# An mLSTM cell and a mixture of depths on one core: gates on 96 partitions, other places in a step, another order of the tail

## The chip, the core and the metric

The kernel runs on one core of one Trainium2 chip, in float32. A core has five engines that run their own instruction streams: TensorE (PE, matmuls into PSUM), VectorE (DVE), ScalarE (ACT), GpSimd (POOL) and SyncE (SP, which here only issues DMAs). The metric is the device time of the kernel in microseconds, the median of several runs; lower is better.

## The reference

Two blocks follow each other. The first is an mLSTM cell over batch 4, 8 heads, 768 positions and head size 40. In each position t it keeps a running maximum m of the gates, a matrix C and a vector n per head:

```python
m_new = np.maximum(f_gate[:, :, t] + m, i_gate[:, :, t])
f_stab = np.exp(f_gate[:, :, t] + m - m_new)
i_stab = np.exp(i_gate[:, :, t] - m_new)
C = f_stab * C + i_stab * outer(v, k)
n = f_stab * n + i_stab * k
y[t] = sigmoid(o_gate[t]) * (C @ q) / max(|n @ q|, 1)
```

The second block is a mixture of depths. Each batch has 768 rows of 8 x 40 = 320 numbers. A score per row (row times w_gate) picks the 128 highest rows of each batch; those alone go through two layers (320 to 1024 with ReLU, 1024 to 320), are scaled by the sigmoid of their score and added to the row. All other rows pass unchanged:

```python
top_idx = np.argpartition(-scores[b], capacity)[:capacity]
h = np.maximum(x[b, top_idx] @ w1, 0.0)
out[b, top_idx] = x[b, top_idx] + sigmoid(scores[b, top_idx])[:, None] * (h @ w2)
```

## The kernel before

**Tiling.** `_fast` (L27) treats 256 positions of one batch as a step: N = 12 steps n, three (s = 0, 1, 2) for each batch b. All 8 heads of a step are done together; inside a step the positions lie in four pieces of 64 (two chunks c of 128 partitions, two halves r). The order of the instructions on each engine is the order in which the program writes them; nothing reorders it. SP, PE, DVE, ACT and POOL each work through their own part of that order and wait for each other by semaphores. `_general` (L614) is a fallback for other numbers and isn't run here.

**A step.** For step n the loop (L524) holds: `load(n + 3)` (L527), DMAs of v, k and q three steps ahead and of o two steps ahead, all on SP; `store(n - 1)` of finished rows to `out`, on SP too; `scores(n)` (L262, PE), `masked(n)` (L274, DVE); `update(n + 1)` (L230, PE, into the one buffer pU), `states(n + 1)` (L242, DVE, running sums of C); `widen` (L202, ACT, spreads q to 64 columns a head); `weigh(n + 2)` (L219, POOL, v times the gate columns into `wv`); `turn` (L206, PE transposes of k or q, ACT copies out of PSUM); `read(n)` (L281, PE, state times q into pH), `attend(n)` (L298, PE, adds scores times `wv` to pH), `divide(n)` (L307, DVE, gives y), `sigmoid` (ACT) and `output(n)` (L320, POOL, y times o into x). `router(n - 1)` (L335, DVE) makes the scores of the second block.

**Gates.** `gate_sums`, `gate_rows`, `gate_cols` (L158, L166, L181) make, for one s, the decays of all 32 pairs of batch and head on 32 partitions: two scans of 256 on DVE, an Exp on ACT, then five small matmuls that turn the rows into columns `cols[s]`. The three s go one after the other: the maximum that one leaves (`m`) starts the next scan. They lie partly ahead of the loop and partly in step 0.

**Second block.** For batch b-1, one batch behind: `spread` (L363, PE and ACT) puts all scores on every partition; `ranks` (L385) counts for each row how many scores are greater, three counts on DVE (`greater`) and three on ACT (`signs`); `select` (L413, DVE) makes the one-hot `sel`; `numbers` (L451, PE `pi`, then DVE `index`) turns it into row numbers; `fetch` (L459) gathers these rows from `out` by an indirect DMA on POOL, and `fetched` (L466) transposes them; `layer1` (L480), `layer2` (L491, ending with the scaled copy `yg` on ACT and an indirect DMA on POOL that adds `yg` to `out`). In a batch's step s = 1 there are ranks, select, numbers and fetch of the batch before (and layer 2 of the one before that); in s = 2 there are fetched and layer 1. The last batch takes its rows with a one-hot matmul from x in SBUF (`picked`, L429), and its counts are made in two parts (`ranks_first`, `ranks_last`), because its last third comes late.

**Tail.** After the loop: score of the last step, layers of batch 2, ranks, `picked`, layers of batch 3. Just before layer 2 of batch 3 all engines read a flag `good` (L608) that decides on the fallback.

**PSUM.** Pools `ps_s` (one buffer of two banks: scores, spread), `ps_u` (one of two banks: pU), `ps_t` (two of one bank: transposes, `ph`, `py`, `pi`, `pX`, gate columns), `ps_h` (one of two banks: pH).

Of the kernel before, what the change touches and what calls it, by code (L numbers as in the profile page):

```python
# [16 lines left out]
BIG = 1.0e30  # L17
# [9 lines left out]
def _fast(ctx, tc, q, k, v, i_gate, f_gate, o_gate, w_gate, w1_in, w2_in, out):  # L27
# [11 lines left out]
    WARM = 18  # L39
# [16 lines left out]
    f_sb = gate.tile([BH, S], FP, name="f_sb")  # L56
    i_sb = gate.tile([BH, S], FP, name="i_sb")

    def load(n):

        if n < N:
            b, s = divmod(n, NS)
            for t, src in ((v_t, v), (k_t, k)):
                for c in range(2):
                    a = s * 256 + c * 128
                    SP.dma_start(out=t[n % NB][:, c, :, 0:D], in_=src[b, :, a:a + 128, :].rearrange("h p d -> p h d"))
            SP.dma_start(out=q_t[n % NB], in_=q[b, :, 256 * s:256 * s + 256, :].rearrange("h (p t) d -> p h (t d)", t=2))
        n -= 1
        if 0 <= n < N:
            b, s = divmod(n, NS)  # L70
            for r in range(2):
                for c in range(2):
                    a = s * 256 + c * 128 + r * 64
                    SP.dma_start(out=o_t[n % NO][64 * c:64 * c + 64, r],
                                 in_=o_gate[b, :, a:a + 64, :].rearrange("h p d -> p h d"))

    SP.dma_start(out=f_sb, in_=f_gate.rearrange("b h s -> (b h) s"))
    SP.dma_start(out=i_sb, in_=i_gate.rearrange("b h s -> (b h) s"))
    hot = const.tile([128, 128], FP, name="hot")
    DVE.memset(hot, 1.0)  # L80
    one = gate.tile([BH, 256], FP, name="one")
    DVE.memset(one, 1.0)
    m = gate.tile([BH, NS + 1], FP, name="m")
    DVE.memset(m[:, 0:1], -BIG)
    flags = gate.tile([128, NS + B], FP, name="flags")
# [4 lines left out]
    load(0)  # L90
    wg = const.tile([128, DM], FP, name="wg")
    SP.dma_start(out=wg, in_=_bcast(w_gate, 128))
    load(1)
# [17 lines left out]
    odd = gate.tile([BH, 2], FP, name="odd")  # L111
    for j in range(2):
        DVE.tensor_reduce(out=odd[:, j:j + 1], in_=ident[0:BH, j:BH:2], axis=AX.X, op=OP.add)
    pairs = gate.tile([BH, BH // 2], FP, name="pairs")
    DVE.tensor_tensor(out=pairs, in0=ident[0:BH, 0:BH:2], in1=ident[0:BH, 1:BH:2], op=OP.add)
# [38 lines left out]
    cols = []  # L154

    rowed = {}

    def gate_sums(s):  # L158
        own = slice(256 * s, 256 * s + 256)
        F = gate.tile([BH, 256], FP, name="F", tag="F")  # L160
        a = gate.tile([BH, 256], FP, name="a", tag="a")
        DVE.tensor_tensor_scan(out=F, data0=one, data1=f_sb[:, own], initial=0.0, op0=OP.mult, op1=OP.add)
        DVE.tensor_tensor(out=a, in0=i_sb[:, own], in1=F, op=OP.subtract)
        rowed[s] = F, a

    def gate_rows(s):  # L166
        F, a = rowed[s]
        carry = m[:, s:s + 1]
        M = gate.tile([BH, 256], FP, name="M", tag="M")
        E = gate.tile([BH, 514], FP, name=f"E{s}")  # L170
        DVE.tensor_tensor_scan(out=M, data0=one, data1=a, initial=carry, op0=OP.mult, op1=OP.max)
        DVE.tensor_scalar(out=E[:, 256:512], in0=a, scalar1=M[:, 255:256], scalar2=None, op0=OP.subtract)
        DVE.tensor_tensor(out=E[:, 512:513], in0=carry, in1=M[:, 255:256], op=OP.subtract)
        DVE.tensor_scalar(out=E[:, 0:256].rearrange("b (r c t) -> b c r t", r=2, c=2),
                          in0=M.rearrange("b (c r t) -> b c r t", c=2, r=2), scalar1=M[:, 255:256], scalar2=None,
                          op0=OP.subtract)
        DVE.tensor_tensor(out=m[:, s + 1:s + 2], in0=F[:, 255:256], in1=M[:, 255:256], op=OP.add)
        ACT.activation(out=E[:, 0:513], in_=E[:, 0:513], func=AF.Exp)
        rowed[s] = E

    def gate_cols(s):  # L181
        E = rowed[s]
        dz = gate.tile([BH, 128], FP, name=f"dz{s}")
        DVE.tensor_scalar(out=dz.rearrange("b (j e) -> b j e", j=2), in0=odd.unsqueeze(2).to_broadcast([BH, 2, 64]),
                          scalar1=E[:, 512:513], scalar2=None, op0=OP.mult)
        DVE.tensor_scalar(out=flags[0:BH, s:s + 1], in0=E[:, 0:1], scalar1=LEAST, scalar2=None, op0=OP.is_ge)
        pc = ps_t.tile([128, 5, BH], FP, name="pc", tag="t")
        for j in range(4):
            e = (256, 384, 0, 128)[j]
            PE.transpose(pc[:, j, :], E[:, e:e + 128], ident[0:BH, 0:BH])  # L190
        PE.matmul(pc[:, 4, 0:BH // 2], dz, pairs, start=True, stop=True)
        cols.append(const.tile([128, 5, BH], FP, name=f"cols{s}"))
        DVE.tensor_copy(out=cols[s][:, 0:2, :], in_=pc[:, 0:2, :])  # L193
        for r in range(2):
            DVE.tensor_copy(out=cols[s][:, 2 + r, :].rearrange("s (b j p) -> s b j p", j=2, p=NP),
                            in_=pc[:, 2 + r, :].rearrange("s (b p j) -> s b j p", j=2, p=NP))
        DVE.tensor_copy(out=cols[s][:, 4, 0:BH // 2], in_=pc[:, 4, 0:BH // 2])
# [8 lines left out]
    def turn(n, name):  # L206
        T = work.tile([128, NP, 256], FP, name=name)
        for c in range(2):
            src = k_t[n % NB] if name == "kT" else qw_t[n % 2]
            pt = ps_t.tile([128, NP, 128], FP, name="pt", tag="t")  # L210
            for p in range(NP):
                PE.transpose(pt[:, p, :], src[:, c, 2 * p:2 * p + 2, :].rearrange("s j d -> s (j d)"), ident)  # L212
            if name == "kT":
                ACT.copy(out=T[:, :, 128 * c:128 * c + 128], in_=pt)  # L214
            else:
                ACT.copy(out=T.rearrange("e p (u t) -> e t p u", t=2)[:, c], in_=pt)  # L216
        pending[n][name] = T

    def weigh(n):  # L219
        pending[n] = {}  # L220
        b, s = divmod(n, NS)
        for r in range(2):
            o = slice(64 * r, 64 * r + 64)
            POOL.tensor_tensor(out=wv_t[n % 3][o, :, :, r], in0=v_t[n % NB][o], op=OP.mult,  # L224
                               in1=cols[s][o, 0:2, b * H:b * H + H].unsqueeze(3).to_broadcast([64, 2, H, D1]))
# [193 lines left out]
    def index(b, hi, lo, count):  # L419
# [6 lines left out]
        DVE.tensor_scalar(out=flags[:, NS + b:NS + b + 1], in0=count, scalar1=1.0, scalar2=None, op0=OP.is_equal)  # L426
        dep[b]["idx"] = idx

    def picked(b):  # L429
# [6 lines left out]
        pX = ps_t.tile([128, 3, 128], FP, name="pX", tag="t")  # L436
        d["xeT"] = mod.tile([128, 3, 128], FP, name="xeT")
        for j in range(3):
            for r in range(2 * NS):
                PE.matmul(pX[:, j, :], x[:, r, 128 * j:128 * j + 128], sel[:, r, :], start=(r == 0), stop=(r == 2 * NS - 1))  # L440
            ACT.copy(out=d["xeT"][:, j], in_=pX[:, j])
# [49 lines left out]
    def layer2(b, f0=0, f1=NF):  # L491
# [5 lines left out]
        if f1 < NF:  # L497
            return
        dep.pop(b)
# [7 lines left out]
    gate_sums(0)  # L507
    gate_rows(0)
    gate_sums(1)
    causal()  # L510
    gate_cols(0)
    weigh(0)
    zero(wv_t[2].rearrange("s c h r x -> s c h (r x)"))
    zero(k_t[2][:, :, :, D:DP])
    turn(0, "kT")
    gate_rows(1)
    widen(0)
    update(0)
    turn(0, "qT")
    gate_cols(1)  # L520
    weigh(1)
    gate_sums(2)
    scores(0)
    for n in range(N):  # L524
        b, s = divmod(n, NS)
        more = n + 1 < N
        load(n + 3)  # L527
# [8 lines left out]
        if n > 0:  # L536
            scores(n)
        masked(n)
        if n == 0:
            states(0)  # L540
            gate_rows(2)
        if b > 1 and s == 1:
            layer2(b - 2)
        if n > 0 and (s < 2 or not more):
            router(n - 1)
        if b > 0 and s == 1:
            ranks(b - 1)
            select(b - 1)
        if more:
            update(n + 1)  # L550
            states(n + 1, 0, 4 if n else 3)
            widen(n + 1)
        if n > 0 and n + 2 < N:
            weigh(n + 2)
        if n > 0 and s == 2 and more:
# [3 lines left out]
        if not more:  # L559
            sigmoid(n)  # L560
            gated(n)
        read(n)
        if b > 0 and s == 1:
            numbers(b - 1)
            fetch(b - 1)
        if n == 0:
            gate_cols(2)
            states(1, 3)
            weigh(2)
            tables()  # L570
        if more:
# [4 lines left out]
            if b > 0 and s == 2:  # L576
                fetched(b - 1)
                layer1(b - 1, 0)
                layer1(b - 1, 4)
        else:  # L580
            dep[b] = {"sb4": spread(b, 0, 4)}
            ranks_first(b)
        attend(n)
        divide(n)
        if more:
            output(n)
        if n == 1:
            margins()
    b = B - 1
    router_last(N - 1)  # L590
    output(N - 1)
    fetched(b - 1)
    layer1(b - 1, 0)
    ranks_last(b)
    store(N - 1)
    layer1(b - 1, 4)
    layer2(b - 1)
    picked(b)
    layer1(b, 0)
    layer1(b, 4)  # L600
    picked_numbers(b)
    good = gate.tile([1, 1], I32, name="good")
    pg = ps_s.tile([1, NS + B], FP, name="pg", tag="s")
# [3 lines left out]
    DVE.tensor_scalar(out=good, in0=total, scalar1=float(NS * BH + 128 * B), scalar2=None, op0=OP.is_equal)  # L607
    value = nc.values_load(good[0:1, 0:1], min_val=0, max_val=1)  # L608
    layer2(b)
# [352 lines left out]
```

## Time and profile before

| | us |
|---|---|
| median of 3 runs | 196.38 |
| lowest and highest | 194.38, 197.03 |
| the profiled execution | 198.05 |
| its span, first to last instruction | 196.1 |
| PE busy | 157.8 |
| DVE busy | 106.2 |
| ACT busy | 77.9 |
| POOL busy | 72.0 |

The span is divided on the page into 40 slices of 4.9 us, with one digit for each: the busy share of an engine in tenths, or the clock granted to PE. A line of a timeline gives start, duration, engine, line of the program, operation, output and input, how many instructions are merged, and in brackets how long the engine stood idle before and what ended that. A matmul in float32 shows as two records. The loads have short rows: of 93606 DMA packets 88352 are under 512 bytes. The DMA queue of SP carries 22.65 MB. The chain of work that ended last is 57% PE, 9% ACT, 8% DMA and 7% DVE.

### The profile page before, as it was taken

How to read it: one execution, taken by the hardware profiler on the slowest of the kernel's cores; microseconds unless marked ns; L12 is line 12 of the kernel's file. 1: busy time of each engine (PE TensorE's matmuls, PEld its weight loads, DVE VectorE, ACT ScalarE, POOL GpSimd, SP SyncE). 2: the span in 40 equal slices, each digit the busy share in tenths (PEclk: the TensorE clock that was granted, in tenths of full speed). 3: DMA queues.
4: the chain of work that ended last, by engine and by line, in shares of the span. 5: the costliest groups of instructions: out<-in, count | busy, mean ns of one | idle time of the engine just before them, and what ended most of it. 6: DMA issues, size and time to landing. Idle time of an engine off the chain costs nothing.

```text
span 196.1 us, 6660 instructions
## 1 busy us (share of the span) xinstructions
PE 157.8 (80%) x2857; PEld 138.3 (71%) x2857; DVE 106.2 (54%) x269; ACT 77.9 (40%) x142; POOL 72.0 (37%) x89
## 2 busy tenths in 40 slices
PE   7866499998972980899996998999958759989650
PEld 7765489987961870899975787998748559779420
DVE  5747857869598255008796293297855583200100
ACT  8731158553761331132519534242463445211110
POOL 4235029699362026205335480092312540030030
PEclk9975589999996698599999699999988979999996
DMA  5999999859788978998799889720221202020002
GB/s 110 197 183 149 184 181 156 158 120 178 161 137 183 301 126 169 310 192 163 126 165 188 163 202 156 157 67 5 70 33 37 70 4 62 5 33 0 7 10 37
DMA packets 93606, 24.31 MB, mean 124 GB/s; under 512 B 88352, under 2 KB 93088, under 8 KB 93568
## 3 DMA queue, kind: packets, MB, share of 16 engines
q1 hardware_dynamic: 92848, 22.65, 61.0%
q0 software_dynamic: 720, 1.15, 3.6%
q8 instruction: 24, 0.39, 0.9%
q14 instruction: 14, 0.11, 0.2%
HBM read 19.20 MB, written 4.59 MB: 121 GB/s over the span
## 4 chain that ended last, share of the span: by engine, by line
PE 57%; issue 9%; ACT 9%; DMA 8%; DVE 7%; SPq 4%; POOL 2%; POOLq 0%; ACTq 0%; DVEq 0%
PE ph L487 13%; PE pt L212 9%; PE py L496 7%; PE pH L303 7%; PE pU L238 5%; PE pS L271 4%; ACT sgn L383 4%; DMA v<-in_v_dram 4%; PE pH L293 3%; PE warm L89 3%; DMA xe<-out_dram,idx 3%; PE pX L440 2%; PE pB L368 2%; DMA o<-in_o_gate_dram 2%; POOL wv L224 1%
## 5 line engine op out<-in xcount | busy, mean ns | idle before, releaser
L224 POOL TENSOR_TENSOR wv<-v,cols 64x656 f32<-64x656 f32 x24 | 34.3, 1428 | 25.7 <-DVE cols L193 19.6
L325 POOL TENSOR_TENSOR x<-y,o 128x320 f32<-128x320 f32 x24 | 20.7, 882 | 42.4 <-issue 18.8
L487 PE MATMUL ph<-xeT,w 128*128 128x128 f32 x192 | 26.4, 304 | 4.2 <-ACT xeT L472 4.2
L487 PEld LDWEIGHTS ph<-xeT,w 128*128 128x128 f32 x192 | 25.6, 218 | 5.2 <-ACT xeT L472 5.1
L340 DVE CUSTOM_DVE_ANT_0 scr<-x,wg 128x320 f32<-128x320 f32 x22 | 22.4, 1018 | 4.7 <-POOL x L325 3.0
L238 PE MATMUL pU<-wv,k 128*64 128x82 f32 x384 | 17.7, 249 | 7.0 <-issue 4.2
L216 ACT COPY qT<-pt 128x512 f32<-128x512 f32 x24 | 14.2, 628 | 21.3 <-PE pt L212 21.2
L238 PEld LDWEIGHTS pU<-wv,k 128*64 128x64 f32 x384 | 15.6, 146 | 8.9 <-issue 5.3
L312 DVE SCALAR_TENSOR_TENSOR den<-pH,cols 128x16 f32<-128x16 f32 x12 | 2.1, 175 | 35.8 <-PE pH L303 35.8
L214 ACT COPY kT<-pt 128x512 f32<-128x512 f32 x24 | 13.0, 585 | 20.6 <-PE pt L212 20.5
L496 PE MATMUL py<-w,hT 128*128 128x320 f32 x64 | 18.2, 437 | 1.0 <-DVE good L607 1.0
L303 PE MATMUL pH<-wv,P 128*64 128x82 f32 x384 | 18.8, 258 | 0.0
L502 POOL DMA_INDIRECT out_dram<-yg,idx x4 | 6.3, 1585 | 33.7 <-ACT yg L501 30.7
L303 PEld LDWEIGHTS pH<-wv,P 128*64 128x64 f32 x384 | 16.8, 155 | 2.2 <-issue 1.5
L212 PE MATMUL pt<-ident,qw 128*128 128x128 f32 x96 | 16.9, 322 | 1.8 <-DVE flags L426 0.7
L496 PEld LDWEIGHTS py<-w,hT 128*128 128x128 f32 x64 | 11.8, 190 | 5.6 <-issue 1.0
L212 PEld LDWEIGHTS pt<-ident,qw 128*128 128x128 f32 x96 | 12.1, 161 | 3.9 <-PE pt L212 1.7
L271 PE MATMUL pS<-qT,kT 40*64 40x64 f32 x768 | 14.8, 229 | 0.0
L293 PE MATMUL pH<-C,qT 40*64 40x41 f32 x704 | 13.9, 229 | 0.9 <-DVE y L317 0.6
L277 DVE TENSOR_TENSOR P<-pS,mask 128x1024 f32<-128x1024 f32 x12 | 14.6, 1213 | 0.0
L293 PEld LDWEIGHTS pH<-C,qT 40*64 40x64 f32 x704 | 12.4, 134 | 3.0 <-issue 2.3
L250 DVE TENSOR_TENSOR C<-pU,C 128x164 f32<-128x164 f32 x40 | 13.1, 326 | 1.9 <-PE pU L238 0.8
(106 smaller groups left out, 214.2 us busy)
## 6 DMA issues: line engine op xcount, KB each, us to landing
v<-in_v_dram SPq DMA_DIRECT2D x24, 160.0 KB, 4.2
k<-in_k_dram SPq DMA_DIRECT2D x24, 160.0 KB, 4.9
q<-in_q_dram SPq DMA_DIRECT2D x12, 320.0 KB, 5.6
o<-in_o_gate_dram SPq DMA_DIRECT2D x48, 80.0 KB, 3.6
out_dram<-x SPq DMA_DIRECT2D x24, 160.0 KB, 3.1
w<-in_moe_w_dram SPq DMA_DIRECT2D x1, 1280.0 KB, 7.4
w<-in_moe_w_dram SPq DMA_DIRECT2D x2, 512.0 KB, 5.9
w<-in_moe_w_dram SPq DMA_DIRECT2D x1, 256.0 KB, 7.2
```

The source lines that it names most:

```text
L212: PE.transpose(pt[:, p, :], src[:, c, 2 * p:2 * p + 2, :].rearrange("s j d -> s (j d)"), ident)
L216: ACT.copy(out=T.rearrange("e p (u t) -> e t p u", t=2)[:, c], in_=pt)
L224: POOL.tensor_tensor(out=wv_t[n % 3][o, :, :, r], in0=v_t[n % NB][o], op=OP.mult, in1=cols[s][o, 0:2, b * H:b * H + H].unsqueeze(3).to_bro ...
L238: PE.matmul(pU[64 * j:64 * j + 64, c, p], k_t[n % NB][:, c, 2 * p + j, :], wv_t[n % 3][:, c, 2 * p + j], start=True, stop=True)
L271: PE.matmul(pS[o, j, c, p, :], kT[e, p, t], qT[e, p, t], start=True, stop=True)
L277: DVE.tensor_tensor(out=P.rearrange(flat), in0=pending[n].pop("pS").rearrange(flat), op=OP.mult, in1=mask.unsqueeze(1).to_broadcast([128, ...
L293: PE.matmul(g["pH"][64 * c:64 * c + 64, NP * j + p, r], g["qT"][e, p, t], state[n, 2 * c + r][e, p, :], start=(c, j) not in g["begun"], st ...
L303: PE.matmul(g["pH"][64 * c:64 * c + 64, NP * j + p], g["P"][:, j, c, p, :], wv_t[n % 3][:, c, 2 * p + j], start=(c, j) not in g["begun"], ...
L325: POOL.tensor_tensor(out=x.rearrange(order, j=2, d=D), in0=pending[n]["y"][:, r].rearrange("s (j p) d -> s j p d", j=2), in1=o.rearrange(o ...
L340: DVE.tensor_tensor_reduce(out=scr, in0=x[:, r, 0:DM], in1=wg, scale=1.0, scalar=0.0, op0=OP.mult, op1=OP.add, accum_out=x[:, r, DM:DM + 1])
L487: PE.matmul(ph[:, f, :], w1[:, j, (f0 + f) * 128:(f0 + f) * 128 + 128], d["xeT"][:, j, :], start=(j == 0), stop=(j == 2))
L496: PE.matmul(d["py"], d["hT"][:, f, :], w2[:, f, :], start=(f == 0), stop=(f == NF - 1))
```

## The change

*Gates.* f and i are loaded as 96 partitions (three s of 32) in three DMAs each, f on SP and i on ACT. One `gate_rows` without argument makes all three s together; each scan starts fresh, and two small DVE instructions carry the maximum from one group of 32 partitions to the next, which is then taken into account by a maximum in the operations that follow. One `gate_cols` makes the columns of all three.

*Start.* The warm-up matmuls go from 18 to 12. SP loads k, q and v of step 0 in this order instead of v, k, q, then step 1, and w_gate after it. The key transposes of step 0 stand before the gate rows; the second half of `wv` for step 0 is made on DVE. `update(0)` follows `scores(0)` and `masked(0)` inside the loop, `update(1)` follows `read(0)`, `weigh(2)` and `load(3)` lie in step 0, `tables()` at its end.

*Step.* For b = 1, `ranks`/`select` move behind the key transposes, and `numbers`/`fetch` behind `divide`. `layer2` no longer ends with `yg` and the scatter; these are a new `add`, which stands behind `ranks` and `select` in the later batches. `fetched` and `layer1` of the batch before move from the middle of step s = 2 to its end (behind attend, divide and output). The router of s = 1 moves behind `weigh`, except in late batches.

*Tail.* `fetched` and the first half of layer 1 of batch 2 move into step 11. `picked` writes three tiles in three pools with one bank in use of each, instead of one tile. Layer 2 is cut (6 and 2 for batch 2, 4 and 4 for batch 3) and put around other work.

```diff
-    WARM = 18
+    WARM = 12
+    G = NS * BH
+    f_sb = gate.tile([G, 256], FP, name="f_sb")
...
+    for s in range(NS):
+        for e, t, src in ((SP, f_sb, f_gate), (ACT, i_sb, i_gate)):
+            e.dma_start(out=t[BH * s:BH * s + BH], in_=src[:, :, 256 * s:256 * s + 256].rearrange("b h t -> (b h) t"))
...
-    load(0)
+    load_kv(0, k_t, k)
+    load_q(0)
+    load_kv(0, v_t, v)
+    load(1)
     wg = const.tile([128, DM], FP, name="wg")
     SP.dma_start(out=wg, in_=_bcast(w_gate, 128))
-    load(1)
     load(2)
...
+        DVE.tensor_tensor_scan(out=F, data0=one, data1=f_sb, initial=0.0, op0=OP.mult, op1=OP.add)
+        DVE.tensor_tensor(out=a, in0=i_sb, in1=F, op=OP.subtract)
+        DVE.tensor_tensor_scan(out=M, data0=one, data1=a, initial=-BIG, op0=OP.mult, op1=OP.max)
+        for s in range(NS - 1):
+            g, h = slice(BH * s, BH * s + BH), slice(BH * s + BH, BH * s + 2 * BH)
+            DVE.scalar_tensor_tensor(out=m[h], in0=M[g, 255:256], scalar=m[g], in1=F[g, 255:256], op0=OP.max, op1=OP.add)
+        DVE.tensor_tensor(out=top, in0=M[:, 255:256], in1=m, op=OP.max)
+        DVE.tensor_scalar(out=E[:, 256:512], in0=a, scalar1=top, scalar2=None, op0=OP.subtract)
...
+        ACT.activation(out=E, in_=E, func=AF.Exp)
...
-            POOL.tensor_tensor(out=wv_t[n % 3][o, :, :, r], in0=v_t[n % NB][o], op=OP.mult,
+            (DVE if n == 0 and r else POOL).tensor_tensor(out=wv_t[n % 3][o, :, :, r], in0=v_t[n % NB][o], op=OP.mult,
...
-        pX = ps_t.tile([128, 3, 128], FP, name="pX", tag="t")
-        for j in range(3):
+        for j, pX in enumerate((ps_u.tile([128, 2, 512], FP, name="pU"), ps_h.tile([128, 2, 512], FP, name="pX", tag="h"),
+                                ps_t.tile([128, 1, 512], FP, name="pX", tag="t"))):
...
-        if f1 < NF:
-            return
-        dep.pop(b)
+
+    def add(b):
+        d = dep.pop(b)
         yg = mod.tile([128, DM], FP, name="yg")
         ACT.activation(out=yg, in_=d["py"], func=AF.Copy, scale=d["g"])
...
-    gate_sums(0)
-    gate_rows(0)
-    gate_sums(1)
     causal()
-    gate_cols(0)
+    turn(0, "kT")
+    gate_rows()
+    widen(0)
+    gate_cols()
     weigh(0)
+    turn(0, "qT")
...
-        if b > 1 and s == 1:
+        late = b > 1 and s == 1
+        if late:
             layer2(b - 2)
-        if n > 0 and (s < 2 or not more):
+        if n > 0 and (s == 0 or late or not more):
             router(n - 1)
-        if b > 0 and s == 1:
+        if late:
             ranks(b - 1)
             select(b - 1)
+            add(b - 2)
...
-        if not more:
+        else:
             sigmoid(n)
             gated(n)
+        if b == 1 and s == 1:
+            ranks(b - 1)
+            select(b - 1)
         read(n)
-        if b > 0 and s == 1:
+        if late:
             numbers(b - 1)
             fetch(b - 1)
         if n == 0:
-            gate_cols(2)
-            states(1, 3)
-            weigh(2)
-            tables()
+            update(1)
+            states(1)
...
-            if b > 0 and s == 2:
-                fetched(b - 1)
-                layer1(b - 1, 0)
-                layer1(b - 1, 4)
         else:
+            fetched(b - 1)
+            layer1(b - 1, 0)
             dep[b] = {"sb4": spread(b, 0, 4)}
             ranks_first(b)
         attend(n)
         divide(n)
+        if b == 1 and s == 1:
+            numbers(b - 1)
+            fetch(b - 1)
         if more:
             output(n)
...
+        if more and b > 0 and s == 2:
+            fetched(b - 1)
+            layer1(b - 1, 0)
+            layer1(b - 1, 4)
     b = B - 1
     router_last(N - 1)
     output(N - 1)
-    fetched(b - 1)
-    layer1(b - 1, 0)
+    layer1(b - 1, 4)
     ranks_last(b)
     store(N - 1)
-    layer1(b - 1, 4)
-    layer2(b - 1)
+    layer2(b - 1, 0, 6)
     picked(b)
+    layer2(b - 1, 6)
     layer1(b, 0)
+    add(b - 1)
     layer1(b, 4)
     picked_numbers(b)
+    layer2(b, 0, 4)
...
-    layer2(b)
+    layer2(b, 4)
+    add(b)
```

## The prediction

> **What bounds the kernel now.** I read the page's 40 slices first, then the timelines of the SP queue, POOL and PE, then who waited for whom. "Step n" is a pass of the loop with n as its number. The slices:
>
> ```profile
> PE   7866499998972980899996998999958759989650
> PEclk9975589999996698599999699999988979999996
> ```
> ```profile
> DMA  5999999859788978998799889720221202020002
> ```
>
> DMA is busy to slice 25 (126 us), PE almost throughout from slice 16 (80 us), with a granted clock that drops after each hole. The SP timeline, us of start and of issuing:
>
> ```profile
> 60.83 1.64 SPq L531 DMA_DIRECT2D w<-in_moe_w_dram  x3
> 62.56 1.34 SPq L332 DMA_DIRECT2D out_dram<-x  x2
> ```
>
> These are w1's load and store(2). SP issues without pause from 0.8 to 126 us. Until 62 us every buffer it wants has long been free: x(2) was written at 47.6, and store(2) is issued at 62.56 because SP got there only then. So this stream runs by itself, ahead of no engine. POOL, then PE:
>
> ```profile
> 72.01 1.25 POOL L462 DMA_INDIRECT xe<-out_dram,idx  x1 [11.96 <-DVE C L258]
> ```
> ```profile
> 78.06 0.87 PE L470 MATMUL pX<-ident,xe 128*128 128x128 f32 x3 [4.89 <-DMA xe<-out_dram,idx]
> 79.50 7.74 PE L487 MATMUL ph<-xeT,w 128*128 128x128 f32 x48 [0.57 <-ACT xeT L472]
> 87.17 1.36 PE L303 MATMUL pH<-wv,P 128*64 128x82 f32 x32
> 107.16 0.30 PE L456 MATMUL pi<-place,sel 128*128 128x3 bf16 x6 [1.54 <-DVE sel L415]
> 109.75 2.07 PE L303 MATMUL pH<-wv,P 128*64 128x82 f32 x32
> 159.14 4.52 PE L487 MATMUL ph<-xeT,w 128*128 128x128 f32 x24 [2.66 <-ACT xeT L472]
> 172.79 1.60 PE L440 MATMUL pX<-sel_f,x 128*128 128x128 f32 x12 [0.35 <-ACT xeT L441]
> ```
>
> The gather of batch 0 reads rows of `out`, so it needs the batch's stores. The releaser named can't be it (what it needs of DVE, `idx`, was written at 63.1); by the trace's landings store(2) lands at 70.9, behind w1's 1280 KB, and the gather starts at 72.01. Its rows land at 77.9 and free PE. So **two regimes**: to 78 us the DMA stream decides, through that gather; from 78 on PE's own order decides, with holes that the last lines show.
>
> **What the Trainium skill says.** "VectorE: DVE Perf Modes", Why tensor_reduce can't reduce along partition axis: each partition lane is a pipeline of its own. So I let 96 partitions cost what 32 do; the trace has no 96-row scan. "SBUF — State Buffer", Who interferes with whom: a VectorE instruction with two SBUF inputs and a GpSimd one that reads SBUF exclude each other. It agrees: the M scan took 0.74 alone and 1.77 beside `wv`, the router product 0.49 and 1.13. "DMA: Bandwidth & Descriptors", Issuing engines are not separate DMA queues: gate loads on ACT's queue save issue time only; nothing here shows a load from ACT. "TensorE: Matmul & The Clock Gate", The HAM clock gate: an idle window of about 3.4 us halves the clock. It agrees: after the 4.9 us hole layer 1 took 7.74, later 5.62.
>
> **Part 1, the start: about 9 us earlier, worth nothing at the end.** Removed: two of three rounds of gate rows on DVE (F 0.7, a 0.4, M 0.7, E 1.0: 2.9 us alone, up to 6.4 beside POOL), two Exp of 0.63, two rounds of transposes and copies, and 12 warm records (2.1). Added: two 0.14 links, one 0.14 maximum, and one round whose column copies are three times as wide (some 1 us). On SP three f loads replace f and i, one issue of 0.4 more; i goes to ACT, three issues of about 0.4, ahead of its table load and zero fills. These delay the fills, done by 6.8 instead of 5.4 and 7.9 with the third. Bounds for the 96-row round: 2.9 us, or three times that. The half of `wv`(0) on DVE lies between 0.8 (the y product) and 1.8 (locked out by POOL). Keys come before v: k(0) lands near 6 instead of 7.3, and its two ACT copies now stand ahead of Exp. I get columns near 10 (8.5 before), scores(0) near 12 (16.0), and states(0) without gate_sums(2) (3.1) before it, so update(1) near 16 instead of 22.2 and attend(0) near 20 instead of 29.3.
>
> Then PE runs into the loads: q(4), q(5), q(6) land at 40.6, 51.3, 60.8 whatever PE does. So attend(3), (4), (5) end near 44, 56, 66. In step 4 ranks(0) moves behind the key transposes, numbers and gather behind divide; the 4.2 us wait for `sel` becomes one near 58. All this is covered by store(2) at 70.9: with 12 us in hand at attend(5), bounds of Part 1 (even 6 us worse) change nothing. POOL still has the gather ahead of output(4), so router(4), and DVE behind it, wait to 75 as before.
>
> **Part 2, attend(5) before layer 1: 1.3 us.** Layer1(0) now follows attend(5), which is done when the rows land. Layer 1 still starts near 79.5, cold, 7.7 us. Then scores(6) starts, not attend(5): 1.29 gained. Bounds: 0, if the longer hole costs as much clock; 3, if store(2) comes earlier.
>
> **Part 3, steps 7 and 10: 2.7 each, 5.4.** The `yg` copy waited on ACT for layer 2 (done 102.2) with three signs behind it (3.2 us), then `cnt`, `sel`, `pi`. With add() behind select, the signs run during layer 2. DVE's router and three counts then set `sel`, 2.9 us earlier. PE without holes needs: scores 1.09, layer 2 4.52, pU 1.28, kT 1.02, read 1.07, pi 0.2, qT 1.05, attend 1.29: 11.5. The second qT half still waits for `idx`, est. 0.9: 12.4 against 15.17 (96.58 to 111.75). The scatter on POOL moves behind the signs with `yg`; layer 2 still times it, so weigh(9)'s second half, which waits for its landing, is no later. Bounds 1.5 to 3.5.
>
> **Part 4, step 8: 0.5.** Layer1(1) behind attend(8): of 1.2 us of holes (qT copy, xeT copy) half is left. The gather lands about 113, PE comes at 115.
>
> **Part 5, step 11 and tail: 5.0.** From scores(11) to the last py: 149.26 to 188.78, 39.5. By rows, hole-free: scores 1.1, read 1.1, pB 1.5, attend 1.3, xe 0.5, layer 1 twice 10.9, layer 2 twice 9.0, pX 4.4, pi and pg 0.5: 30.3. So 9.2 of holes and half clock. What goes: the xeT copy no longer stands behind four signs (2.66) and layer1(2) isn't cold (1.8; half now lies before attend); three banks remove two 0.35; layer2's last two f hide the last copy. What remains or is new: y 0.5, xeT 0.5, `sel_f` about 0.6 (DVE: two counts 1.5, three 1.5, adjusting 0.6), `good` 1.0 (four f now cover pi and flags), and a new one: py(2) holds one of two slots until add(), so the last ph waits for a copy, 0.6 to 1.1. Sum about 4.2 instead of 9.2. Bounds 2.5 to 6.5. The end behind py (yg, scatter, landing: 7.3) stays.
>
> **Sum.** 1.3 + 5.4 + 0.5 + 5.0 = 12.2. The profiled execution took 198.05 (span 196.1 and 1.95 around it); it becomes 185.9. It stood 1.67 over the median of 196.38, so the median becomes about 184.2; I write **184.5**.
>
> **Rivals.**
> - *The loop gives its part back* (0.17): sel isn't late by ACT alone; DVE's router waits for POOL's output, so pi waits as before. For it: router ran with 1.13 beside POOL. Against: DVE stood 1.75 us waiting for the signs. Then 1.3 + 5.0: 190.1, or 189 to 193.
> - *The gate opens* (0.10): SP gets to store(2) some 4 to 8 us earlier, since fewer things compete in the queue, and Part 1 pays. Against: the bytes in the stream are the same, and no wait on SP before 62 is long (largest 1.7). 176 to 180.
> - *Slower through the clock* (0.06). Place: PE waits 12 us instead of 5 before layer1(0), and starves in each early step. Price: the path from 79 to 189 has about 98 us left on PE at a mean granted clock near 0.93. It ends over 2% slower when that stretch is 16 us longer, a mean of 0.80; each hole of 4 to 5 us costs about 2.1 (7.74 less 5.62), so seven more holes decide. Against: Parts 3 and 5 remove holes. Then 200 to 206.
> - *The edits don't bite* (0.04): slots chosen so that `pX` and ph wait on each other, 192.5 to 198.
>
> **Chances.** The forecast keeps 0.63, with its own range 181 to 188. Two per cent (192.45 and 200.3), about what a measurement of this kernel can tell from no change, is the bound. Faster 0.63 + 0.10 + most of the first rival, 0.12: 0.85. Same 0.05 + 0.04: 0.09. Slower 0.06. The range 179 to 192 takes in the forecast, most of the first rival and a little of the second.
>
> **What would show it.** attend(0) ending near 20 and attend(5) before 68, a hole until about 78, and the gather still at 72: Part 1 worth nothing. scores(6) near 87; scores(8) near 108 and scores(11) near 142, with `sel` before read's end; from scores(11) to the last py under 36; span near 184. It is wrong if the gather of batch 0 moves by more than 2 us, if pi in steps 7 and 10 waits over 1 us, or if the stretch from 79 shows a clock under 0.88.

## The result, and the profile after

| us | before | after |
|---|---|---|
| median (lowest to highest), 4 runs each | 196.7 (194.38 to 197.25) | 189.25 (188.12 to 191.2) |
| the profiled execution | 198.05 | 188.54 |
| its span | 196.1 | 186.6 |

The ratio is 0.9623, with a 95% interval of 0.9509 to 0.9738: faster, with a gain of 7.45 us. The forecast was 184.5 (179 to 192), 4.75 us too low. The ratio leaves out one execution of the changed kernel, 191.2, as it is more than 1.5% above the fastest; the medians hold all.

The slices of the page after, each 4.7 us, counted from 1 (digits as before):

```profile
PE   7679886999586891599999598999988899998740
PEclk9978999699969788559999999999999579999995
DMA  4998998998999998999797998774141300200203
```

PE is busier early (it runs ahead until the loads stop it), then there is the same gap in slices 16 and 17 (70 to 79 us) with a half clock behind it, and a second dip of the clock in slice 32 (145 to 149 us) in which PE itself shows no long hole. Below, work at half clock is called cold and work at full clock warm. The SP timeline and the POOL line of the gather of batch 0 (start, duration, line, what moves):

```profile
60.66 1.75 SPq L534 DMA_DIRECT2D w<-in_moe_w_dram  x3
62.51 1.34 SPq L341 DMA_DIRECT2D out_dram<-x  x2
```
```profile
71.41 1.25 POOL L471 DMA_INDIRECT xe<-out_dram,idx  x1 [11.00 <-DMA v<-in_v_dram]
```

The store is issued within 0.05 us of where it was and the gather 0.6 us from where it was, although scores(0) now starts at 11.7 instead of 16.0 and attend(0) ends at 21.4 instead of 30.6. The PE timeline, in the order of the lines shown of before:

```profile
69.17 1.36 PE L312 MATMUL pH<-wv,P 128*64 128x82 f32 x32
...
75.96 0.87 PE L479 MATMUL pX<-ident,xe 128*128 128x128 f32 x3 [5.43 <-DMA xe<-out_dram,idx]
77.41 8.54 PE L496 MATMUL ph<-xeT,w 128*128 128x128 f32 x48 [0.57 <-ACT xeT L481]
85.88 1.16 PE L280 MATMUL pS<-qT,kT 40*64 40x64 f32 x64
...
93.99 1.16 PE L280 MATMUL pS<-qT,kT 40*64 40x64 f32 x64
...
104.51 0.30 PE L465 MATMUL pi<-place,sel 128*128 128x3 bf16 x6 [1.48 <-DVE sel L424]
...
106.64 1.36 PE L312 MATMUL pH<-wv,P 128*64 128x82 f32 x32
...
129.57 1.16 PE L280 MATMUL pS<-qT,kT 40*64 40x64 f32 x64
...
138.55 0.30 PE L465 MATMUL pi<-place,sel 128*128 128x3 bf16 x6
...
146.65 5.39 PE L496 MATMUL ph<-xeT,w 128*128 128x128 f32 x24 [0.57 <-ACT xeT L481]
...
162.53 2.84 PE L449 MATMUL pX<-sel_f,x 128*128 128x128 f32 x24
```

attend(5) (69.17) now lies ahead of layer 1, so scores(6) follows layer 1 at once. The row numbers `pi` come without a wait in step 10 (138.55), but still with one of 1.48 in step 7 (104.51). Half of layer 1 of batch 2 lies in step 11 and takes 5.39 for 24 records; the other half, same count, took 2.94 at 154.16. `pX` has lost its 0.35 waits.

By the starts of scores, the 9.5 us of span divide as follows: scores(6) 2.6 earlier (88.46 to 85.88); step 7 shorter by 1.2 (15.17 to 13.94; under "Add back" it turns out that this is the clock and not the order); step 8 by 0.7 (14.2 to 13.5); step 10 by 3.1 (15.2 to 12.1); scores(11) to the last py by 1.9 (39.5 to 37.6). Steps 6 and 9 and the end behind py are as they were.

### The profile page after: what moved, and what is told of

Read it like the earlier page. It is cut to its first block, busy times and chain, and to the rows that moved or that the text cites. A ratio compares the mean times of both kernels' runs of the same rounds, so it can differ in the third digit from the quotient of the medians.

```text
span 186.6 us, 6586 instructions
## 1 busy us (share of the span) xinstructions
PE 154.2 (83%) x2833; PEld 135.9 (73%) x2833; DVE 94.6 (51%) x245; ACT 77.3 (41%) x140; POOL 68.3 (37%) x88
## 5 line engine op out<-in xcount | busy, mean ns | idle before, releaser
L233 POOL TENSOR_TENSOR wv<-v,cols 64x656 f32<-64x656 f32 x23 | 30.4, 1323 | 36.2 <-DMA v<-in_v_dram 29.7
L496 PE MATMUL ph<-xeT,w 128*128 128x128 f32 x192 | 28.3, 317 | 2.4 <-ACT xeT L481 1.7
L496 PEld LDWEIGHTS ph<-xeT,w 128*128 128x128 f32 x192 | 27.3, 230 | 3.9 <-ACT xeT L481 2.7
L247 PE MATMUL pU<-wv,k 128*64 128x82 f32 x384 | 19.4, 264 | 6.0 <-POOL wv L233 6.0
L247 PEld LDWEIGHTS pU<-wv,k 128*64 128x64 f32 x384 | 17.2, 158 | 7.8 <-POOL wv L233 6.4
L349 DVE CUSTOM_DVE_ANT_0 scr<-x,wg 128x320 f32<-128x320 f32 x22 | 16.4, 744 | 8.3 <-POOL x L334 6.7
L223 ACT COPY kT<-pt 128x512 f32<-128x512 f32 x24 | 13.0, 586 | 15.6 <-PE pt L221 15.5
L259 DVE TENSOR_TENSOR C<-pU,C 128x164 f32<-128x164 f32 x40 | 13.1, 327 | 6.9 <-PE pU L247 5.8
L312 PE MATMUL pH<-wv,P 128*64 128x82 f32 x384 | 16.3, 237 | 0.0
L213 ACT COPY qw<-q 128x640 f32<-128x640 f32 x12 | 8.7, 722 | 17.5 <-DMA q<-in_q_dram 17.5
L505 PEld LDWEIGHTS py<-w,hT 128*128 128x128 f32 x64 | 11.7, 190 | 5.7 <-issue 1.0
L312 PEld LDWEIGHTS pH<-wv,P 128*64 128x64 f32 x384 | 14.4, 136 | 1.8 <-issue 1.2
L221 PE MATMUL pt<-ident,k 128*128 128x128 f32 x96 | 15.3, 308 | 0.3 <-DMA k<-in_k_dram 0.3
L302 PE MATMUL pH<-C,qT 40*64 40x41 f32 x704 | 14.5, 232 | 0.9 <-DVE y L326 0.9
L302 PEld LDWEIGHTS pH<-C,qT 40*64 40x64 f32 x704 | 12.9, 138 | 3.1 <-issue 1.9
L221 PE MATMUL pt<-ident,qw 128*128 128x128 f32 x96 | 13.6, 280 | 1.7 <-DVE flags L435 1.3
```

What stands on the lines that cost most here:

```text
L233: (DVE if n == 0 and r else POOL).tensor_tensor(out=wv_t[n % 3][o, :, :, r], in0=v_t[n % NB][o], op=OP.mult, in1=cols[s][o, 0:2, b * H:b * ...
L247: PE.matmul(pU[64 * j:64 * j + 64, c, p], k_t[n % NB][:, c, 2 * p + j, :], wv_t[n % 3][:, c, 2 * p + j], start=True, stop=True)
L302: PE.matmul(g["pH"][64 * c:64 * c + 64, NP * j + p, r], g["qT"][e, p, t], state[n, 2 * c + r][e, p, :], start=(c, j) not in g["begun"], st ...
L312: PE.matmul(g["pH"][64 * c:64 * c + 64, NP * j + p], g["P"][:, j, c, p, :], wv_t[n % 3][:, c, 2 * p + j], start=(c, j) not in g["begun"], ...
L349: DVE.tensor_tensor_reduce(out=scr, in0=x[:, r, 0:DM], in1=wg, scale=1.0, scalar=0.0, op0=OP.mult, op1=OP.add, accum_out=x[:, r, DM:DM + 1])
L496: PE.matmul(ph[:, f, :], w1[:, j, (f0 + f) * 128:(f0 + f) * 128 + 128], d["xeT"][:, j, :], start=(j == 0), stop=(j == 2))
```

## The experiments

The theory of the prediction: the gather of batch 0 is held by store(2), so the start is worth nothing; behind it PE's order decides, and the gain is in steps 7, 10 and the tail. The rivals were a start that pays, a move that the loop gives back, and a clock that takes its share. All edits below are made on the changed kernel unless the text says otherwise. "Tail" is scores(11) to the last py in the profile.

| | median (lowest to highest) | before beside it | step 7 | step 10 | tail |
|---|---|---|---|---|---|
| before | 196.7 (194.38 to 197.25) | | 15.2 | 15.2 | 39.5 |
| after | 189.25 (188.12 to 191.2) | 196.7 | 13.9 | 12.1 | 37.6 |
| start only | 196.68 (194.67 to 198.65) | 197.03 | 15.1 | 15.2 | 39.5 |
| store first | 184.83 (182.71 to 185.84) | 197.03 | 17.2 | 12.1 | 36.4 |
| heat | 187.05 (185.61 to 189.52) | 197.03 | 15.0 | 12.2 | 34.8 |
| weigh first | 187.98 (186.87 to 188.23) | 197.03 | 13.1 | 12.2 | 34.8 |
| add back | 188.98 (187.22 to 189.31) | 196.04 | 14.0 | 15.3 | 34.2 |
| layer 1 in mid step | 192.43 (191.99 to 195.25) | 196.04 | 15.5 | 12.1 | 36.2 |
| tail back | 192.83 (192.43 to 195.53) | 196.04 | 15.4 | 12.2 | 40.2 |
| one bank | 189.88 (188.56 to 192.81) | 196.04 | 13.9 | 12.1 | 36.0 |
| after, again | 188.88 (184.16 to 189.36) | 196.91 | 15.5 | 12.1 | 35.9 |
| add back, again | 189.72 (187.53 to 190.85) | 196.91 | 15.4 | 15.1 | 34.2 |
| store first, weigh(8) late | 186.77 (184.08 to 190.53) | 196.91 | 12.9 | 12.2 | 37.6 |
| the same with heat | 186.56 (182.97 to 187.29) | 196.91 | 15.7 | 12.2 | 34.7 |

The medians of the kernel before agree within 1 us from row to row, though its single executions reach from 192.81 to 201.09; so differences of 2 us and more between rows are read, and those below 1 us are not. The last three columns are of one profile each. Step 7 and the tail differ by more than 1.5 us between two profiles of one and the same kernel (after: 13.9 and 15.5, 37.6 and 35.9), by where a half clock falls.

**Start only.** The new gates and start, with the order of the loop and of the tail as before (this diff is against the kernel before):

```diff
-    gate_sums(0)
-    gate_rows(0)
+    turn(0, "kT")
+    gate_rows()
+    widen(0)
+    gate_cols()
...
```

> The kernel before with the new start alone: gates on 96 partitions, 12 warm-up matmuls, the order of the first loads, and the new step 0. Steps 1 to 11 and the tail stand as before. My theory (the gather of batch 0 waits for store(2), which the DMA stream brings at about 71 us whatever PE does): attend(0) ends near 21 instead of 30.6, but the gather starts at 71 to 73 and layer 1 of batch 0 at 77 to 80 as before; time within 1.5 us of the kernel before (196.7). Rival (the start passes through to the end): 187 to 188.

The time is that of before. PE of this kernel at the gather:

```profile
77.83 0.87 PE L479 MATMUL pX<-ident,xe 128*128 128x128 f32 x3 [5.05 <-DMA xe<-out_dram,idx]
```

It stands 0.23 us from its place before (78.06), with scores(0) at 11.3 instead of 16.0. The start is worth nothing by itself, and the whole gain belongs to the order of the loop and the tail.

**Store first.** If store(2) is the gate, moving it ahead of load(6) must open it:

```diff
+        if n == 3:
+            store(2)
         if more:
             load(n + 3)
...
-        if n > 0:
+        if n > 0 and n != 3:
             store(n - 1)
```

> The changed kernel with store(2) put on SP ahead of load(6), o(5) and w1 instead of behind them; same bytes, same number of DMAs. My theory: the gather is held by that store alone, so it starts within 2 us of the row numbers (63.2), its rows land at 67 to 70, scores(6) starts at 79 to 81 instead of 85.9, and the time falls by 4 to 7 us, to 182.5 to 185. Rival A (the stream's bytes hold PE here, not this store): less than 1 us. Rival B (w1 becomes the last to arrive): layer 1 waits for w1 until 70 to 74 and 2 to 4 us are gained.

The gate opened: SP issues store(2) at 53.5 and the gather leaves at 63.83. POOL, then PE, of this kernel:

```profile
63.83 1.25 POOL L471 DMA_INDIRECT xe<-out_dram,idx  x1 [0.34 <-POOL wv L233]
...
88.22 2.64 POOL L233 TENSOR_TENSOR wv<-v,cols 64x656 f32<-64x656 f32 x2 [9.09 <-DMA v<-in_v_dram]
```
```profile
71.91 5.62 PE L496 MATMUL ph<-xeT,w 128*128 128x128 f32 x48 [0.57 <-ACT xeT L481]
...
97.80 0.32 PE L465 MATMUL pi<-place,sel 128*128 128x3 bf16 x6 [2.47 <-DVE sel L424]
```

Layer 1 starts 5.5 us earlier and at full clock, and scores(6) 8.4 us earlier. About half of that is lost again: POOL now waits 9.09 us for v(8) before weigh(8), output(6) stands behind it on POOL, router(6) behind that on DVE, then `sel`, and `pi` waits 2.47. Step 7 takes 17.2 (`pi` comes 1.7 later than in after, and a half clock behind it costs the other 1.6), step 8 14.2. The median still falls by 4.4 us to 184.83. **This is the lowest median of all**, 12.2 us under the kernel before beside it, and it shows that this gate held back a gain, though only part of it is to be had. The second rival was close: the last part of w1 landed at 71.6, just ahead of layer 1. What the same move gives with the old start wasn't tried.

**Heat.** The half clock could be the price in layer 1. Matmuls that nothing reads were put ahead of the two cold places: three behind scores(11), two behind `fetched` in step 11, sixteen behind output(5).

```diff
+    def heat(n):
+        t = ps_u.tile([128, 2, 512], FP, name="pU")
+        for i in range(n):
+            PE.matmul(t[:, i % 2, 0:128], hot, hot, start=True, stop=True)
...
+        if not more:
+            heat(3)
...
+            heat(2)
...
+        if n == 5:
+            heat(16)
```

> The changed kernel with matmuls whose result nobody reads in PE's holes: 16 ahead of the transposes of the gathered rows in step 5, 3 behind scores(11), 2 behind the transposes of step 11. My theory (the holes before layer 1 of batch 0 and in step 11 let the granted clock fall to a half): layer 1 of batch 0 takes 5.6 to 6 instead of 8.5, the first half of layer 1 of batch 2 takes 2.8 instead of 5.4; time 184 to 186 instead of 189.25. Rival (the clock falls for another reason, or these matmuls stand in the way): both durations stay, 189 to 191.

PE of this kernel around layer 1 of batch 0:

```profile
68.25 3.84 PE L214 MATMUL pU<-hot 128*128 128x128 f32 x32
76.14 0.87 PE L484 MATMUL pX<-ident,xe 128*128 128x128 f32 x3 [4.05 <-DMA xe<-out_dram,idx]
77.59 7.75 PE L501 MATMUL ph<-xeT,w 128*128 128x128 f32 x48 [0.57 <-ACT xeT L486]
```

The sixteen were done 4 us before the rows came, and layer 1 was cold (7.75) all the same: this half missed. In step 11 the five did what was expected: 2.9 for the first half of layer 1, and a tail of 34.8. The median, 187.05, is 2.2 us below after's, but above the 184 to 186 that were expected.

**Weigh first.** Step 7 kept its wait, by the theory because `cnt` on DVE met `wv` on POOL. These are the two timelines of after, DVE and POOL:

```profile
101.53 1.94 DVE L399 TENSOR_SCALAR cnt<-cnt 128x3 f32<-128x3 f32 x1
103.50 0.96 DVE L424 TENSOR_TENSOR sel<-iota,cnt 128x768 bf16<-128x768 f32 x1
...
137.09 0.16 DVE L399 TENSOR_SCALAR cnt<-cnt 128x3 f32<-128x3 f32 x1
```
```profile
101.59 1.83 POOL L233 TENSOR_TENSOR wv<-v,cols 64x656 f32<-64x656 f32 x1
```

An instruction on three numbers a partition takes 1.94 and ends 0.05 after `wv`; in step 10, where no `weigh` runs, it takes 0.16. The edit puts weigh(9) ahead of the scatter on POOL:

```diff
         if late:
             ranks(b - 1)
             select(b - 1)
+            if n + 2 < N:
+                weigh(n + 2)
             add(b - 2)
...
-        if n + 2 < N:
+        if n + 2 < N and not late:
             weigh(n + 2)
```

> The changed kernel with weigh(9) on POOL ahead of the scatter of batch 0 in step 7 instead of behind it. My theory (the small cnt operation on DVE took 1.94 us there, since it and POOL's product exclude each other): cnt takes 0.2, sel is ready 1.5 us earlier, PE's wait for pi (1.48) goes, step 7 lasts 12.4 to 12.8 instead of 13.9; time 1 to 1.5 us lower, about 188. Rival (the product now excludes the router's product or the scatter, and nothing is gained): step 7 stays within 0.4 of 13.9.

DVE of this kernel:

```profile
100.24 1.34 DVE L349 CUSTOM_DVE_ANT_0 scr<-x,wg 128x320 f32<-128x320 f32 x1
...
104.56 0.26 DVE L399 TENSOR_SCALAR cnt<-cnt 128x3 f32<-128x3 f32 x1
```

`cnt` falls to 0.26, so the collision is shown. But the router's second product now takes 1.34 beside POOL instead of 0.49, so `pi` comes only 0.8 earlier and step 7 gains only 0.8. Step 8 is 1.2 longer, nearly all of it in holes of scores(8) for which the profile shows no wait; whether they come from the edit is open. The total, 187.98, has a warm tail in its profile and can't be told from that of after.

**Add back.** Part 3 alone undone: `add` directly behind `layer2` again.

```diff
         if late:
             layer2(b - 2)
+            add(b - 2)
...
             select(b - 1)
-            add(b - 2)
```

> The changed kernel with add() directly behind layer 2 again in steps 7 and 10, so that its yg copy stands on ACT ahead of the three signs. My theory (the signs behind yg set sel in these steps): step 10 lasts 15 instead of 12.1, step 7 lasts 15 instead of 13.9; time 4 us higher, 193. Rival (sel is set by DVE's own counts): both steps within 0.5 us of the changed kernel.

Step 10 grew by 3.2 to 15.3; step 7 (14.0) did not change, though 15 had been expected. Yet the total was that of after, and not the 193 that had been expected. Since the tail of this profile was warm and after's was not, both kernels ran once more, side by side:

> The changed kernel once more, beside the next run on the same chip. In its first profile the first half of layer 1 of batch 2 ran at half clock (5.4 us for 24 records), in four of the experiments at full clock (2.9) with that part unchanged. If the clock there hangs on where a fixed window falls, another profile can show either; expected from scores(11) to the last py: 34 to 35 where it is 2.9, 36.5 to 38 where it is 5.4; time 187.5 to 190.

> The same edit as e5, which made step 10 3.2 us longer and yet left the time. My theory now: the step is paid for, and the first reading lay in the spread of the clock at the tail (34.2 us there against 37.6); beside the changed kernel on one chip it is 1.5 to 3 us slower. Rival (the time isn't set by step 10, since the tail takes back what the step lost): within 1 us of the changed kernel.

189.72 against 188.88: less than the 1.5 to 3 us that the theory asked for, so by its own measure the rival held. Step 10 is 15.1 against 12.1, so the move is worth 3.0 where it stands; the tail is 34.2 against 35.9. ACT, then PE, of the second add-back kernel show the three late signs that hold `pi`:

```profile
137.48 0.53 ACT L510 ACTIVATE yg<-py,g 128x320 f32<-128x320 f32 x1 [6.15 <-PE py L505]
137.91 0.93 ACT L392 ACTIVATE sgn<-sb,x 128x768 f32<-128x768 f32 x1
...
140.86 0.19 ACT L392 ACTIVATION_READ_ACCUMULATOR sgn<-sb,x 128x1 f32 x1
```
```profile
142.30 0.30 PE L465 MATMUL pi<-place,sel 128*128 128x3 bf16 x6 [1.53 <-DVE sel L424]
...
150.75 2.94 PE L496 MATMUL ph<-xeT,w 128*128 128x128 f32 x24 [0.57 <-ACT xeT L481]
```

In both add-back profiles the halving falls ahead of layer 1 (142.4 to 145.9, and 144.5 to 147.9 with layer 1 from 150.75), which then takes 2.94. In both profiles of after the halving falls on layer 1 (5.39 and 4.3). So the tail gives part of the step's 3 us back. As a time Part 3 isn't shown: over ten executions of each kernel the mean is 189.2 with `add` back and 188.6 without, a difference that the spread doesn't separate from none.

The same profiles show what is order and what is clock in steps 7 and 10. PE of before, then of "after, again", the second profile of after (its scores(7) starts at 95.25):

```profile
96.58 1.16 PE L271 MATMUL pS<-qT,kT 40*64 40x64 f32 x64
...
134.05 1.16 PE L271 MATMUL pS<-qT,kT 40*64 40x64 f32 x64
...
144.64 0.30 PE L456 MATMUL pi<-place,sel 128*128 128x3 bf16 x6 [1.54 <-DVE sel L415]
...
147.22 2.11 PE L303 MATMUL pH<-wv,P 128*64 128x82 f32 x32
```
```profile
105.78 0.30 PE L465 MATMUL pi<-place,sel 128*128 128x3 bf16 x6 [1.48 <-DVE sel L424]
...
108.36 2.45 PE L312 MATMUL pH<-wv,P 128*64 128x82 f32 x32
```

In step 10 `pi` comes 10.59 after scores(10) before, and 8.97 or 8.98 in every profile with `add` behind `select`. Behind `pi`, step 10 ran in part at half clock in all four profiles with the old order (before, start only, add back twice) and in none of the ten others; that is the other 1.5 of the 3 us. In step 7 `pi` comes 10.58 after scores(7) before, 10.58 and 10.59 with `add` back, and 10.52 and 10.53 in the two profiles of after. The order gave nothing there. The 1.2 by which step 7 is shorter in the first profile of after lies behind `pi`: attend(7) took 2.07 before, 1.36 in the first profile of after, and 2.45 in the second, whose step 7 takes 15.5.

**Layer 1 in mid step.** Parts 2 and 4 alone undone (steps 5 and 8):

```diff
+            if b > 0 and s == 2:
+                fetched(b - 1)
+                layer1(b - 1, 0)
+                layer1(b - 1, 4)
...
         attend(n)
...
-        if more and b > 0 and s == 2:
-            fetched(b - 1)
-            layer1(b - 1, 0)
-            layer1(b - 1, 4)
```

> The changed kernel with fetched and layer 1 of steps 5 and 8 ahead of attend again. My theory: scores(6) starts 1.3 us later (attend comes behind layer 1), step 8 is 0.5 us longer; time 1.5 to 2 us higher, 191. Rival (the longer hole ahead of layer 1 costs as much clock as attend saves): within 0.5 us.

3.2 us slower than after, more than expected. scores(6) starts 1.7 later than in the first profile of after, but 0.5 later than in the second (87.14), whose step 7 takes 15.5 too; step 8 takes 1.5 longer than in both, with a half clock from 106.4 to 113.2. So the cost is shown as a time, but only in part where it arises.

**Tail back.** Part 5 alone undone: all of layer 1 of batch 2 behind the loop, one tile for `picked`, layer 2 undivided.

```diff
-            fetched(b - 1)
-            layer1(b - 1, 0)
             dep[b] = {"sb4": spread(b, 0, 4)}
...
-    layer1(b - 1, 4)
+    fetched(b - 1)
+    layer1(b - 1, 0)
     ranks_last(b)
     store(N - 1)
-    layer2(b - 1, 0, 6)
+    layer1(b - 1, 4)
+    layer2(b - 1)
+    add(b - 1)
     picked(b)
...
```

> The changed kernel with the old tail: fetched and all of layer 1 of batch 2 behind the loop, picked in one tile of one bank, layer 2 undivided. My theory: from scores(11) to the last py 39 to 40 instead of 37.6, since the xeT copy waits again behind four signs (2.7) and the three copies of picked are seen again (0.7), while the cold first half of layer 1 of batch 2 is there in both; time 2 us higher, 191. Rival (the tail's new order was worth the 5 us that I forecast): 194.

3.6 us slower than after, with a tail of 40.2, 2.6 above after's; the first half of layer 1 of batch 2 is cold again (4.45 for 24 records). The three parts undone singly cost 3.2 (2 and 4), 3.6 (5) and under 1 us (3), together about the 7.45 that were gained.

**One bank.** Only `picked` goes back to one tile:

```diff
-        for j, pX in enumerate((ps_u.tile([128, 2, 512], FP, name="pU"), ps_h.tile([128, 2, 512], FP, name="pX", tag="h"),
-                                ps_t.tile([128, 1, 512], FP, name="pX", tag="t"))):
+        pX = ps_t.tile([128, 3, 128], FP, name="pX", tag="t")
+        for j in range(3):
```

> The changed kernel with picked in one tile of one bank again, all else as changed. My theory: PE waits 0.35 us twice for the copies, and a little more where the slots shift; picked takes 5 to 5.4 instead of 4.2; time 0.5 to 1.2 us higher. Rival (the copies are hidden anyway): no difference in picked.

0.6 us above after, which the spread doesn't separate from none. In the profile the tail is 36.0 with a warm layer 1, against 34.8 in the two profiles (heat, weigh first) that are warm too: 1.2 for the banks.

**Store first, weigh(8) late.** Can the 3 us that store first lost in step 7 be had back, by taking weigh(8) from in front of output(6)?

```diff
-        if n + 2 < N:
+        if n + 2 < N and n != 6:
             weigh(n + 2)
...
             output(n)
+        if n == 6:
+            weigh(n + 2)
```

> store(2) ahead of load(6) as in e2, and in step 6 weigh(8) on POOL behind output(6) instead of ahead of it. In e2 output(6) stood behind weigh(8), which waited for v(8) until 88.2, so router(6) and with it sel came late and step 7 took 17.2 us. My theory: step 7 takes 13.8 to 14.5, the gather of batch 1 is earlier, time 182 to 183.5. Rival (the loads themselves bound step 7 and 8 now): step 8 grows by what step 7 loses, time as in e2, 184.8.

Step 7 fell to 12.9, below the expected 13.8 to 14.5. Step 8 grew to 22.0, and there the rival held. SP, POOL, then PE of this kernel:

```profile
102.13 1.53 SPq L341 DMA_DIRECT2D out_dram<-x  x2
```
```profile
106.64 1.07 POOL L471 DMA_INDIRECT xe<-out_dram,idx  x1 [5.57 <-DMA v<-in_v_dram]
```
```profile
111.66 0.88 PE L479 MATMUL pX<-ident,xe 128*128 128x128 f32 x3 [4.78 <-DMA xe<-out_dram,idx]
113.11 7.40 PE L496 MATMUL ph<-xeT,w 128*128 128x128 f32 x48 [0.57 <-ACT xeT L481]
```

By its times it is the gate of batch 0 over again, one batch later: SP issues store(5) at 102.13, it lands at 105.6, the gather of batch 1 leaves at 106.64 and its rows land at 111.5; PE has a hole until then, and layer 1 behind it is cold. This wasn't tested by moving store(5). The same kernel with the five unread matmuls of step 11:

> e11 and 3 unread matmuls behind scores(11), 2 ahead of layer 1 of batch 2, in holes of 0.85 and 0.57 us. My theory (these holes can let the clock fall for the next window): from scores(11) to the last py at most 35 us in the profile, time 0 to 2 us under e11 and less spread. Rival (the holes don't decide): no difference to e11.

The tail is warm (34.7), but the time, 186.56, can't be told from 186.77: step 7 ran in part at half clock (98.5 to 101.9) and took 15.7.

## Why the prediction was right or wrong

**Right in the gate and in most places of the gain, wrong in step 7, too large in its sum.** The side was as forecast; of 12.2 us, 9.5 came in the span. Luck went both ways in these 9.5: this one profile gives Part 2 and step 7 more than the order does, and Part 5 less.

- *Part 1, worth nothing.* Held, by its own signs (attend(0) ends at 21.4, gather at 71.41) and by start only and store first. 96 partitions do cost what 32 do: the scan F took 0.69 on 96 rows, 0.68 before on 32.
- *Part 2, 1.3.* It gave 2.6. The extra is the rows' landing, at 75.8 instead of 77.9, less a layer 1 that is colder (8.54 instead of 7.74). The bound of 3 held it. The extra is chance: in the eight profiles with this order and store(2) in its old place scores(6) starts at 85.3 to 88.1, on average at 86.7, and in the three with layer 1 ahead of attend(5) at 88.0, which makes 1.3.
- *Part 3, 2.7 for each step.* Step 10 gave 3.1, half of it the wait for `sel` and half the clock behind it. Step 7 gave nothing: the 1.2 in the profile is clock. **The mis-sized term** is `sel` in step 7, 2.7 for a gain of 0.06 at `pi`. The prediction saw that the signs would no longer be last; it didn't ask what `cnt` then meets. It meets weigh(9) on POOL: 1.94 instead of 0.17, which uses up the 1.75 that DVE had stood waiting for the signs. The rule that it took from the skill, two SBUF inputs against a GpSimd read, doesn't cover an instruction with one input. Another sentence of the same section does ("SBUF — State Buffer", Who interferes with whom): `tensor_scalar` can, under conditions, enter modes with two ports, and then one of the two engines fully blocks the other. Weigh first agrees (0.26 without `wv` beside it); in which mode `cnt` ran, no trace says. So the first rival held for one of the two steps, by `cnt` and not by the router.
- *Part 4, 0.5.* It gave 0.7.
- *Part 5, 5.0.* It gave 1.9 in this profile and 3.9 on average (35.86 over the eight profiles with this tail and without unread matmuls, 39.75 over the three with the old one); undoing it cost 3.6 in time. The waits were sized about right (`sel_f` 0.33 for 0.6, last ph 0.69 for 0.6 to 1.1, no `pX` waits). **The second mis-sized term** is the clock: layer 1 of batch 2 was counted warm, since it no longer followed a wait of 2.66, and half of it cost 5.39 instead of 2.9. With the halving elsewhere, the tails of heat, weigh first and both add-back runs are 34.2 to 34.8: the forecast of 34.5 is what the order gives at full clock. A slip is in it too: what the prediction lists as left over adds up to 3.2 to 3.7, not 4.2.
- *From span to median.* The profile of before stood 1.67 over its median, and the forecast took that off. The profile of after stood 0.71 under its own. This is 2.4 of the 4.75 us; the span is 2.7 (186.6 for 183.9), and rounding up to 184.5 takes 0.3 back.
- *The rivals.* The gate did not open by itself (store(2) at 62.51). When it was opened, the kernel fell to 184.83, not into the 176 to 180 that was worked out, for the loads of v(8) then decided step 7. The clock didn't make the kernel slower, but layer 1 of batch 2 at half clock (5.39 for 2.9) is, beside step 7, the largest piece of what is missing in the span.
- *Its signs.* attend(0), the gather, scores(8) (107.93) and scores(11) (141.71) came as said, and from 79 us on the mean clock is 0.93. Two signs of being wrong or short did come: `pi` waits 1.48 in step 7, and the tail takes 37.6, not under 36. attend(5) ends at 70.5, not before 68, so the hole ahead of layer 1 of batch 0 is 5.4 us and not 12.

## What to carry to other kernels

Look for the wait that a long in-order queue imposes on something far away: here one store behind a weight load of 1280 KB in SP's stream made a start that was 9 us earlier worth nothing, and moving that store ahead was worth over 4. When an operation is moved, look at what its neighbours on the other engines do at its new time, the tiny ones too. And count a matmul after short holes as half-clocked in one of the bounds, unless the profile shows it warm in more than one execution. For the same reason, before a shorter step is put down to an edit, look whether the instruction that the edit frees comes earlier, and whether a second profile of the same kernel is as short.

## What the runs showed of the hardware

**Half clock without a long hole.** Four windows of after, each 3.4 us (length, then busy us and number of records of PE, its weight loads, DVE, ACT and POOL, then granted clock, DMA share, GB/s):

```profile
138.20:141.60 3.40, 2.88 (x76) 2.46 (x67) 1.38 (x8) 2.06 (x4) 0.67 (x1) 1.00 0.42 48
141.60:145.00 3.40, 2.55 (x134) 2.22 (x130) 2.52 (x6) 0.80 (x2) 1.37 (x3) 1.00 0.20 53
145.00:148.40 3.40, 2.83 (x26) 2.35 (x18) 3.06 (x7) 0.61 (x2) 2.88 (x3) 0.50 0.39 93
148.40:151.80 3.40, 3.40 (x18) 3.40 (x18) 0.00 (x0) 0.07 (x1) 0.00 (x0) 0.50 0.04 9
```

The prediction read the skill as asking for an idle window. Here PE was busy for 2.55 of 3.4 us, its largest hole 0.85, and the next two windows ran at half. The Trainium skill also says ("TensorE: Matmul & The Clock Gate", What's actually happening) that the window of 3413 ns is free-running; the traces agree, as in each of the 14 profiles the halvings lie on one grid of 3.413 us whose offset differs from execution to execution. That fits the spread: the first half of layer 1 of batch 2 took 2.9 in 6 profiles and 4.3 to 5.5 in 5, with nearly the same instructions ahead of it. Busy time alone isn't the rule, since the window of after from 104.0 had 2.1 us and kept the clock. The work ahead of the fall was scores and read, on 40 of 128 rows. Over all 581 full-clock windows of the 14 profiles from 10 us on, the best threshold of busy time is wrong for 19, and for 9 if the matmuls on 40 rows are counted at 40/128 of their time; this is a fit made afterwards, and no run tested it.

**Unread work ahead of a gap.** Sixteen matmuls that ended 4 us ahead changed nothing; five in the last 3.4 us ahead of layer 1 of batch 2 had a warm layer behind them in both kernels with them. Without them 4 of 9 profiles were warm, so two say little for the five.
